# The first fifty microseconds of a Fourier-mixing and ReGLU kernel, put in another order: filter loads, first products, inverse copies

## The chip, the cores and the metric

The kernel runs on one core of a Trainium2 chip. The metric is device time in microseconds (us), the median of the runs; less is better. Three runs of the kernel before gave 865.61, 865.96 and 867.79 us, so its median is 865.96 us. One of its executions was also taken by the hardware profiler; all durations below come from that one.

## What is computed

```python
def _attn_ref(x, filt_r, filt_i):
    X = np.fft.rfft(x, axis=1)              # x: 8 batches, 3008 positions, 256 channels
    F = (filt_r + 1j * filt_i)[None, :, :]  # 1505 frequencies, 256 channels
    Y = X * F
    return np.fft.irfft(Y, n=x.shape[1], axis=1)

def _moe_ref(x, w_gate, w_val, w_out):      # 24064 tokens, 256 -> 1536 -> 256
    gate = np.maximum(x @ w_gate, 0.0)
    val = x @ w_val
    return gate * val @ w_out
```

All inputs and the output are float32.

## The kernel before

**The Fourier part.** The length 3008 is split as 94 x 32 (`N1`, `N2`), and both transforms are small matrix products. For each batch:

- *Stage A* contracts the 94 rows with the table `WA`, in float32. `x` stands in two tiles `XF[0]` and `XF[1]` of 16 columns n2 each, loaded in quarters (`load_x`, L185 to L192; one quarter of a batch is three DMAs of 256 KB). One call of `a_bank` (L260, the matmul is L265) fills one PSUM bank `psA`. Batch 0 uses `a_0` (copies at L277 into `AS0`), batch 1 uses `a_1`. One call of `a_1` is named an *item* below (L651); there are 16 of them, four for each quarter of `x`, and its copies (L290) go to `AS1`.
- A transpose turns the 32 columns n2 into partitions. For batch 0 VectorE does it (`turn_0`, L303, four quarters, the instruction is L300) and the result is the tile `at`. Half of batch 1 goes through DRAM (`store_half`, `load_half`), the other half through VectorE (`turn_1`).
- `fwd(b, i)` (L402) is the second forward product: 16 matmuls fill two banks `psX` (e = 0 and 1). There are six blocks i.
- `product(b, i, e, k)` multiplies such a bank by a filter: k = 0 is the real filter `Ftr` and gives `tt`, k = 1 is the imaginary filter `Fti` and gives `uu`. VectorE does it from PSUM (L422). For three blocks (`ON_POOL`, e = 1 of i = 0, 1, 2) ScalarE copies the bank to `xs` (L419) and GpSimd multiplies (L420).
- `inv(b, q)` (L445) takes the products of blocks 2q and 2q + 1 to four banks `psD`, 64 matmuls for batch 0; there are three. It needs the tables `I2t` and `I2u`, which the kernel makes from `F2` (`make_back_t`, `make_back_u`). For batch 0 the banks are copied into `DS0` (L458) and `turn_d(0)`, `turn_d(1)` (L316) transpose them into `D0`, half of the channels each.
- `item_c(k, h)` (L538) is the last inverse product for 512 tokens and one half h of the channels; its copy (L544 or L546) gives `yT`.

**The feed-forward part** runs over 47 blocks of 512 tokens. `gv` (L555) makes value and gate, ScalarE copies the value (`vsb`, L558), VectorE makes the product with the rectified gate (`prod`, L560), and `o_part` (L576) contracts with `WoT`, copies (L589) and stores (L600). The transforms of batches 1 to 7 are strewn among these blocks by a table of step numbers (`at_step`). The first `gv` needs all of the batch 0 transform.

**What sets the order.** The instructions stand in the order in which the Python calls them; no scheduler moves them. Each engine runs its own queue in order. The eight PSUM banks are handed out in rotation in program order (`bank`, `done`), so an instruction that takes a bank waits for the copy that freed it. DMAs issued by SyncE (SP), and those issued by GpSimd (POOL), rotate over eight semaphores each, so the ninth waits for the first.

**The front.** `load_filters` (L226) issues 16 DMAs on GpSimd in four groups of four: mirrored rows of `Ftr` (L231), mirrored rows of `Fti`, direct rows of `Ftr` (L236), direct rows of `Fti`. After stage A of batch 0, a small DMA `hold` (L647) reads `Ftr[0:2, 4, 0:8]`. It stands in SP's queue ahead of all of batch 1's `x` (L648), so this `x` starts when a mirrored and a direct part of `Ftr` have landed. `first_b` (L472) then mixes forward blocks, products, inverses and items, with filler matmuls (`warm`, L607, 128x512 on a tile of ones). What follows it is short:

```python
    first_b(item)
    ...
    for h in range(2):
        turn_d(h)
    item(7)
    for hh in range(2):
        item_c(0, hh)
    item(3)
    turn_1(0)
```

**The end.** In the last block, `o_part` copies each group of 128 tokens (t = 0 to 3) to a free part of `XF`: VectorE copies t = 1 and 2, and the last group is shared, channels 0 to 127 by VectorE (L585) and the others by ScalarE (L586). Each group is stored by two or three runs of rows, issued by GpSimd (t = 0) or by SP and ScalarE in turn; runs are cut at a multiple of 16 rows into two DMAs (`cut`, L596).

Of the kernel before, what the change touches and what calls it, by code (L numbers as in the profile page):

```python
# [116 lines left out]
def kernel(  # L117
# [18 lines left out]
    W = 512  # L136
# [89 lines left out]
    def load_filters():  # L226

        for src, dst in FILT:
            for c in range(4):
                r, k1, n = 32 * c + 1, 1 + H * c, H - c // 3  # L230
                nc.gpsimd.dma_start(dst[r:r + 31:2, :n, :],  # L231
                                    _ap(src, (N1 - k1) * D, [[N1 * D, 16], [-D, n], [1, D]]))
        for src, dst in FILT:
            for c in range(4):
                r, k1, n = 32 * c, 1 + H * c, H - c // 3
                nc.gpsimd.dma_start(dst[r:r + 31:2, :n, :], _ap(src, k1 * D, [[N1 * D, 16], [1, n * D]]))  # L236
# [31 lines left out]
    def a_0(n2, nn, d0, nd):  # L268

        psA = a_bank(n2, nn, d0, nd)  # L270
        dq = D // 4
        l, q = n2 % NC2, slice(d0 // dq, (d0 + nd) // dq)
        c = n2 // NC2
        dst = AS0.rearrange("p q (l c) e (g f) -> p l c g q e f", c=2, g=2)[:, l:l + nn, c // 2, c % 2]
        src = psA.rearrange("p n (q e f) -> p n q e f", e=dq // 2, f=2)
        for i in range(nd // dq):
            nc.scalar.copy(dst[:, :, q.start + i], src[:, :, i])  # L277
        done(psA)
# [19 lines left out]
    def turn_pairs(dst, src):  # L298

        nc.vector.transpose(dst.bitcast(FP32).rearrange("p k c g -> p c k g"),  # L300
                            src.bitcast(FP32).rearrange("p n c g -> p c n g"))

    def turn_0(q):  # L303
        w = D // 8
        turn_pairs(ats[0][:, :, q * w:q * w + w], AS0[:, q])

# [80 lines left out]

    ON_POOL = ((0, 1), (1, 1), (2, 1))
    ats = {}
# [45 lines left out]
    def inv(b, q):  # L435
# [3 lines left out]
        for m in range(2):  # L439
            for k in range(last + 1):  # L440
                for r in range(2):
                    for c in range(4):
                        for e in range(2):
# [5 lines left out]
                                             tile_position=(32 * c, 64 * e))  # L449
        dst = sb.tile([128, 8, D], BF16, tag="dsb", bufs=3, name="dsb") if b else DS0  # L450
        def out(cs):
            for c in cs:
                copy = nc.vector.tensor_copy if (c % 2 if b else (q, c) in ((1, 3), (2, 0), (2, 1))) else nc.scalar.copy
                if b:
                    copy(dst[:, c:8:4, :], psD[c])
                else:
                    k, g = 4 * q + c // 2, c % 2 * 2
                    copy(dst[:, k:k + 3:2, :, g:g + 2], psD[c].rearrange("p m (f e) -> p m e f", f=2))  # L458
                done(psD[c])
        if not b:  # L460
            return out(range(4))

# [9 lines left out]
    def first_b(item):  # L472

        def products(i, es=(1, 0)):
            for e in es:
                for k in range(2):
                    product(0, i, e, k, pool=(i, e) in ON_POOL)

        for i in range(3):
            fwd(0, i)  # L480
            if i < 2:
                products(i)
        make_back_u()
        products(2)
        warm(3)
        fwd(0, 3)
        products(3, (1,))
        warm(3)
        fwd(0, 4)
# [42 lines left out]
    def item_c(k, h):  # L532
# [35 lines left out]
    def o_part(blk, s, prods):  # L568
# [9 lines left out]
        if s in (5, 11) or last and s % 3 == 2:  # L578
# [3 lines left out]
            else:  # L582
                osb = fs.tile([128, 2, D], FP32, tag="osb", bufs=4)
            if s == 11 and last:
                nc.vector.tensor_copy(osb[:, 1, 0:D // 2], psO[:, 1, 0:D // 2])  # L585
                nc.scalar.copy(osb[:, 1, D // 2:], psO[:, 1, D // 2:])  # L586
            else:
                copy = nc.vector.tensor_copy if last else nc.scalar.copy
                copy(osb[:, t0 % 2:t % 2 + 1], psO[:, t0 % 2:t % 2 + 1])  # L589
# [172 lines left out]
```

## Time and profile before

| What | Value |
|---|---|
| Three runs, median | 865.96 us |
| The profiled execution, its own time | 865.68 us |
| Its span, first to last instruction | 863.8 us (1.9 us lie around it) |
| TensorE matmuls busy | 848.7 us, 98% of the span |
| VectorE, ScalarE, GpSimd busy | 577.8, 494.6, 458.4 us |
| Stage A of batch 0 ends on TensorE | 20.3 us |
| First `gv` matmul | 45.6 us |
| Last matmul ends | 858.2 us |

Engines are written PE (TensorE matmul), PEld (its weight loads), DVE (VectorE), ACT (ScalarE), POOL (GpSimd) and SP (SyncE); a q behind the name (SPq, ACTq) means that the engine issues a DMA. A row of a timeline has the start in us, the length in us, engine, line, operation, output tile <- input tiles, shape, count, and in brackets the idle time before it and what ended it. Rows of equal instructions that follow each other are merged. A row of the chain of waits has start, length, and what the end of the program waited for then. A row of stages has the stretch, its length, then the busy time of PE, PEld, DVE, ACT and POOL with counts, the granted TensorE clock as a share of full speed, the share of time the 16 DMA engines were busy, and GB/s.

### The profile page before, as it was taken

How to read it: one execution, taken by the hardware profiler on the slowest of the kernel's cores; microseconds unless marked ns; L12 is line 12 of the kernel's file. 1: busy time of each engine (PE TensorE's matmuls, PEld its weight loads, DVE VectorE, ACT ScalarE, POOL GpSimd, SP SyncE). 2: the span in 40 equal slices, each digit the busy share in tenths (PEclk: the TensorE clock that was granted, in tenths of full speed). 3: DMA queues.
4: the chain of work that ended last, by engine and by line, in shares of the span. 5: the costliest groups of instructions: out<-in, count | busy, mean ns of one | idle time of the engine just before them, and what ended most of it. 6: DMA issues, size and time to landing. Idle time of an engine off the chain costs nothing.

```text
span 863.8 us, 20396 instructions
## 1 busy us (share of the span) xinstructions
PE 848.7 (98%) x7587; PEld 498.8 (58%) x7704; DVE 577.8 (67%) x863; ACT 494.6 (57%) x904; POOL 458.4 (53%) x496
## 2 busy tenths in 40 slices
PE   9999999999999999999999999999999999999997
PEld 4456655656556555556556655565655656666665
DVE  3878865777657775577765787658865688555553
ACT  5765565555655556555555555555556555555552
POOL 6747890488986765776666756767450023000001
PEclk9999999999999999999999999999999999999999
DMA  9985365334782339633386333762464422611111
GB/s 250 241 164 122 96 158 138 109 113 110 190 183 88 84 87 192 166 98 98 85 208 142 95 103 100 190 151 74 101 130 108 99 58 52 126 43 29 37 35 52
DMA packets 101366, 101.61 MB, mean 118 GB/s; under 512 B 21827, under 2 KB 89955, under 8 KB 99730
## 3 DMA queue, kind: packets, MB, share of 16 engines
q1 hardware_dynamic: 81986, 77.96, 36.1%
q0 software_dynamic: 18928, 21.82, 11.7%
q8 instruction: 61, 1.00, 0.5%
q10 hardware_dynamic: 352, 0.52, 0.2%
q14 instruction: 39, 0.32, 0.1%
HBM read 58.23 MB, written 45.88 MB: 121 GB/s over the span
## 4 chain that ended last, share of the span: by engine, by line
PE 94%; DMA 2%; issue 1%; DVE 1%; ACT 1%; SPq 1%; POOL 0%; DVEq 0%; ACTq 0%
PE psG L555 29%; PE psO L576 28%; PE psV L555 26%; PE psA L265 3%; PE psF L367 3%; PE psY L538 3%; PE psD L445 2%; PE psX L402 1%; DMA XF<-in_x_dram 1%; DMA Abuf<-asb 1%; ACT vsb L558 1%; DVE prod L560 1%; SPq L190 0%; DVE tt L422 0%; DMA out_dram<-osb 0%
## 5 line engine op out<-in xcount | busy, mean ns | idle before, releaser
L560 DVE SCALAR_TENSOR_TENSOR prod<-psG,vsb 128x512 bf16<-128x512 f32 x564 | 389.4, 691 | 235.8 <-ACT vsb L558 231.6
L558 ACT CAST vsb<-psV 128x512 bf16<-128x512 f32 x564 | 332.2, 589 | 225.8 <-PE psV L555 121.1
L576 PE MATMUL psO<-WoT,prod 128*128 128x256 bf16 x2256 | 336.6, 273 | 0.8
L555 PE MATMUL psG<-yT,WgT 128*128 128x512 bf16 x1111 | 331.8, 379 | 5.2
L555 PE MATMUL psV<-yT,WvT 128*128 128x512 bf16 x1030 | 314.9, 380 | 0.1
L576 PEld LDWEIGHTS <-prod 128*128 128x128 bf16 x2256 | 220.6, 98 | 143.4
L555 PEld LDWEIGHTS <-WgT 128*128 128x128 bf16 x1128 | 110.0, 97 | 133.5
L432 POOL TENSOR_TENSOR pp<-tt,uu 128x256 bf16<-128x256 f32 x84 | 60.9, 725 | 170.7 <-DVE uu L422 162.5
L555 PEld LDWEIGHTS <-WvT 128*128 128x128 bf16 x1128 | 100.3, 98 | 37.3 <-issue 25.6
L544 ACT CAST yT<-psY 128x512 bf16<-128x512 f32 x93 | 54.5, 586 | 43.2 <-PE psY L538 42.6
L589 ACT COPY osb<-psO 128x512 f32<-128x512 f32 x92 | 54.1, 588 | 22.1 <-PE psO L576 20.7
L600 POOL DMA_DIRECT2D out_dram<-osb x5 | 2.6, 534 | 119.6 <-ACT osb L589 118.0
L422 DVE TENSOR_TENSOR tt<-psX,Ftr 128x512 f32<-128x512 f32 (+1 forms) x93 | 63.5, 683 | 0.5 <-PE psX L402 0.5
L422 DVE TENSOR_TENSOR uu<-psX,Fti 128x512 f32<-128x512 f32 (+1 forms) x93 | 63.3, 681 | 0.3 <-DMA Fti<-in_filt_i_dram 0.3
L433 POOL TENSOR_TENSOR pp<-tt,uu 128x256 bf16<-128x256 f32 x84 | 60.9, 726 | 0.0
L353 POOL TENSOR_TENSOR fold<-XF 128x1024 f32<-128x1024 f32 x24 | 56.3, 2347 | 5.8 <-DMA XF<-in_x_dram 5.4
L354 POOL TENSOR_TENSOR XF<-XF 128x1024 f32<-128x1024 f32 x24 | 56.4, 2350 | 1.9
L257 POOL CAST scr<-prod 128x8 f32<-128x8 bf16 x19 | 3.6, 190 | 85.8 <-DVE prod L560 71.7
L340 POOL DMA_DIRECT2D XF<-in_x_dram x76 | 45.6, 602 | 2.0 <-issue 1.3
L374 ACT CAST asb<-psF 128x512 bf16<-128x512 f32 x48 | 25.8, 589 | 34.5 <-PE psF L367 34.5
L374 DVE CAST asb<-psF 128x512 bf16<-128x512 f32 x48 | 30.9, 686 | 18.0 <-PE psF L367 18.0
L538 PE MATMUL psY<-M,dCb 96*128 96x94 bf16 (+19 forms) x604 | 37.9, 200 | 0.0
(71 smaller groups left out, 457.8 us busy)
## 6 DMA issues: line engine op xcount, KB each, us to landing
Dbuf<-dsb SPq DMA_DIRECT2D x84, 128.0 KB
dCb<-Dbuf SPq DMA_DIRECT2D x56, 192.0 KB
XF<-in_x_dram POOLq DMA_DIRECT2D x38, 256.0 KB, 6.7
Abuf<-asb SPq DMA_DIRECT2D x96, 96.0 KB
at<-Abuf SPq DMA_DIRECT2D x24, 384.0 KB
XF<-in_x_dram SPq DMA_DIRECT2D x31, 256.0 KB
XF<-in_x_dram POOLq DMA_DIRECT2D x76, 96.0 KB, 5.1
out_dram<-osb SPq DMA_DIRECT2D x69, 94.0 KB
```

What stands on the lines that cost most here:

```text
L353: tt(t, xp[:, 0:2], xp[:, 2:4], op=ALU.add)
L354: tt(xp[:, 2:4], xp[:, 0:2], xp[:, 2:4], op=ALU.subtract)
L374: copy(asf[:, :, q, :], banks[q])
L422: nc.vector.tensor_tensor(p, psX, filt, op=ALU.mult)
L432: nc.gpsimd.tensor_tensor(p[:, 0], tt[:, 0], uu[:, 1], op=ALU.subtract)
L433: nc.gpsimd.tensor_tensor(p[:, 1], tt[:, 1], uu[:, 0], op=ALU.add)
L538: nc.tensor.matmul(psY[:, o:o + w], d_rows(b, n2, h), M1[:, 1, n1:n1 + w] if b == 0 else M1[:NROW, 0, n1:n1 + w], start=True, stop=True)
L544: nc.scalar.copy(dst, psY)
L555: nc.tensor.matmul(pt[:, :W], w[:, h, ft * 128:(ft + 1) * 128], yt[:, h, :], start=(h == 0), stop=(h == 1))
L558: nc.scalar.copy(vsb, psV[:, :W])
L560: nc.vector.scalar_tensor_tensor(prod, in0=psG[:, :W], scalar=0.0, in1=vsb, op0=ALU.max, op1=ALU.mult)
L576: nc.tensor.matmul(psO[:, t % 2], prods[ft][:, t * 128:(t + 1) * 128], WoT[:, ft, :], start=(ft == 0), stop=(ft == NFT - 1))
```

## The change

1. `load_filters` issues all of `Ftr` first (mirrored, direct), then all of `Fti`. The number of DMAs stays at 16.
2. The `hold` becomes two. The first reads one element row of `Ftr` that only the first mirrored DMA writes, and the first quarter of batch 1's `x` stands behind it. The second reads `Fti[0:2, 4, 0:8]` (mirrored and direct), and the other three quarters stand behind that.
3. The last `a_0` copy and the last `turn_0` are cut into two halves.
4. `first_b` runs four forward blocks in a row, then all real products, four items, the imaginary products, and fewer filler matmuls (2 instead of 6). The order on TensorE becomes: fwd 0 to 3, four items, filler, fwd 4, an item, inv 0, fwd 5, two items, inv 1, an item, inv 2. GpSimd does its three `tt` before its three `uu`.
5. The copies of inv 0 and inv 1 are all ScalarE's (before, VectorE did one of the four of inv 1 and two of inv 2). The copies of inv 2 are cut in halves of the channels, with VectorE doing two half copies, and each `turn_d` is issued right behind its half.
6. Behind `first_b` come seven items, `item_c(0, 0)` and `(0, 1)`, and one item (before: seven, then three). Each `yT` copy of block 0 is shared: ScalarE the first 256 tokens, VectorE the others.
7. In the last block, VectorE copies the whole last group, and runs of rows are cut only for t = 2 and 3.

```diff
@@ load_filters
                 nc.gpsimd.dma_start(dst[r:r + 31:2, :n, :],
                                     _ap(src, (N1 - k1) * D, [[N1 * D, 16], [-D, n], [1, D]]))
-        for src, dst in FILT:
             for c in range(4):
@@ a_0
         for i in range(nd // dq):
-            nc.scalar.copy(dst[:, :, q.start + i], src[:, :, i])
+            for e in (slice(0, 16), slice(16, 32)) if (n2, d0) == (24, 3 * dq) else (slice(0, 32),):
+                nc.scalar.copy(dst[:, :, q.start + i, e], src[:, :, i, e])
@@ turn_0
-        turn_pairs(ats[0][:, :, q * w:q * w + w], AS0[:, q])
+        n = 2 if q == 3 else 1
+        for i in range(n):
+            e = slice(i * w // n, (i + 1) * w // n)
+            turn_pairs(ats[0][:, :, q * w + e.start:q * w + e.stop], AS0[:, q, :, e])
@@ inv
+        if not b:
+            w = D // 4
+            for h in range(2) if q == 2 else (0,):
+                for c in range(4):
+                    k, g = 4 * q + c // 2, c % 2 * 2
+                    e = slice(h * w, h * w + w) if q == 2 else slice(0, 2 * w)
+                    copy = nc.vector.tensor_copy if (q, h) == (2, 0) and c > 1 else nc.scalar.copy
+                    copy(DS0[:, k:k + 3:2, e, g:g + 2], psD[c].rearrange("p m (f e) -> p m e f", f=2)[:, :, e])
+                if q == 2:
+                    turn_d(h)
+            for c in range(4):
+                done(psD[c])
+            return
...
@@ first_b
+        for i in range(4):
+            fwd(0, i)
+        for k in range(2):
+            for i in range(3):
+                product(0, i, 1, k, pool=True)
         for i in range(3):
-            fwd(0, i)
-            if i < 2:
-                products(i)
+            product(0, i, 0, 0)
+        for e in (1, 0):
+            product(0, 3, e, 0)
+        item(2)
+        for i in range(3):
+            product(0, i, 0, 1)
         make_back_u()
-        products(2)
-        warm(3)
-        fwd(0, 3)
-        products(3, (1,))
-        warm(3)
+        item(2)
+        warm(2)
+        for e in (1, 0):
+            product(0, 3, e, 1)
         fwd(0, 4)
-        item(2)
-        products(3, (0,))
+        item(1)
         inv(0, 0)
         fwd(0, 5)
-        products(4)
-        item(2)
-        products(5)
+        for i in (4, 5):
+            for e in (1, 0):
+                for k in range(2):
+                    product(0, i, e, k)
+            if i == 4:
+                item(2)
         place_own()
         inv(0, 1)
-        item(2)
+        item(1)
         inv(0, 2)
@@ item_c
-        if h == 0 or k:
+        if k:
             nc.scalar.copy(dst, psY)
         else:
-            nc.vector.tensor_copy(dst, psY)
+            nc.scalar.copy(dst[:, :W // 2], psY[:, :W // 2])
+            nc.vector.tensor_copy(dst[:, W // 2:], psY[:, W // 2:])
@@ o_part
-            if s == 11 and last:
-                nc.vector.tensor_copy(osb[:, 1, 0:D // 2], psO[:, 1, 0:D // 2])
-                nc.scalar.copy(osb[:, 1, D // 2:], psO[:, 1, D // 2:])
-            else:
...
-                    cut = w // 16 * 16 if last and not pool else 0
+                    cut = w // 16 * 16 if last and t > 1 else 0
@@ the order of the front
-    hold = sb.tile([2, 8], BF16, tag="hold", bufs=1)
-    nc.sync.dma_start(hold, Ftr[0:2, 4, 0:8])
-    load_x(1, sp, ((0, 0, 2 * q), (0, 2 * q, 4 * q), (1, 0, 2 * q), (1, 2 * q, 4 * q)))
+    for done_by, parts in ((Ftr[1:3:2, 0, 0:8], ((0, 0, 2 * q),)),
+                        (Fti[0:2, 4, 0:8], ((0, 2 * q, 4 * q), (1, 0, 2 * q), (1, 2 * q, 4 * q)))):
+        hold = sb.tile([2, 8], BF16, tag="hold", bufs=2)
+        nc.sync.dma_start(hold[:done_by.shape[0]], done_by)
+        load_x(1, sp, parts)
...
-    for h in range(2):
-        turn_d(h)
     item(7)
     for hh in range(2):
         item_c(0, hh)
-    item(3)
+    item(1)
```

More of the change, by code (lines that the diff above doesn't have):

```diff
@@ L386, in load_at_tiled @@
                               _ap(Abuf[b], rr * N2 * NG * D, [[NG * D, 32], [1, NG * D]]))
-    ON_POOL = ((0, 1), (1, 1), (2, 1))
     ats = {}
@@ L449, in inv @@
                                              tile_position=(32 * c, 64 * e))
-        dst = sb.tile([128, 8, D], BF16, tag="dsb", bufs=3, name="dsb") if b else DS0
+        if not b:
[11 more added lines that the diff above has]
+            return
+        dst = sb.tile([128, 8, D], BF16, tag="dsb", bufs=3, name="dsb")
         def out(cs):
             for c in cs:
-                copy = nc.vector.tensor_copy if (c % 2 if b else (q, c) in ((1, 3), (2, 0), (2, 1))) else nc.scalar.copy
-                if b:
-                    copy(dst[:, c:8:4, :], psD[c])
-                else:
-                    k, g = 4 * q + c // 2, c % 2 * 2
-                    copy(dst[:, k:k + 3:2, :, g:g + 2], psD[c].rearrange("p m (f e) -> p m e f", f=2))
+                copy = nc.vector.tensor_copy if c % 2 else nc.scalar.copy
+                copy(dst[:, c:8:4, :], psD[c])
                 done(psD[c])
-        if not b:
-            return out(range(4))
         def rest():
@@ L472, in first_b @@
     def first_b(item):
[L474 to L477, printed above, removed]
-        for i in range(3):
-            fwd(0, i)
-            if i < 2:
-                products(i)
-        make_back_u()
-        products(2)
-        warm(3)
-        fwd(0, 3)
-        products(3, (1,))
-        warm(3)
+        for i in range(4):
[3 more added lines that the diff above has]
+                product(0, i, 1, k, pool=True)
+        for i in range(3):
+            product(0, i, 0, 0)
[4 more added lines that the diff above has]
+            product(0, i, 0, 1)
+        make_back_u()
+        item(2)
+        warm(2)
+        for e in (1, 0):
+            product(0, 3, e, 1)
         fwd(0, 4)
-        item(2)
-        products(3, (0,))
+        item(1)
         inv(0, 0)
         fwd(0, 5)
-        products(4)
-        item(2)
-        products(5)
+        for i in (4, 5):
[4 more added lines that the diff above has]
+                item(2)
         place_own()
         inv(0, 1)
-        item(2)
+        item(1)
         inv(0, 2)
@@ L583, in o_part @@
                 osb = fs.tile([128, 2, D], FP32, tag="osb", bufs=4)
-            if s == 11 and last:
[L585 to L589, printed above, removed]
+            copy = nc.vector.tensor_copy if last else nc.scalar.copy
+            copy(osb[:, t0 % 2:t % 2 + 1], psO[:, t0 % 2:t % 2 + 1])
             done(psO)
```

## The prediction, on record before the changed kernel ran

> **What bounds the kernel now.** I read the stages first, to find where TensorE is not full.
>
> ```profile
> 20.30:26.80 6.50, 5.18 (x185) 2.49 (x187) 5.71 (x9) 5.60 (x11) 3.10 (x3) 1.00 0.96 269
> 45.60:858.00 812.40, 806.34 (x7102) 478.98 (x7215) 551.40 (x829) 464.42 (x840) 427.54 (x450) 1.00 0.46 111
> 861.50:863.80 2.30, 0.00 (x0) 0.00 (x0) 0.00 (x0) 0.00 (x0) 0.00 (x0) 0.57 0.01 4
> ```
>
> From the first `gv` (45.6) to 858 PE is busy for 806.3 of 812.4 us; the rest is about 1% (records missing from a trace look the same), and the change doesn't touch this stretch. It can only move it, and cut what lies behind it. So the question is when the first `gv` starts, and how long the tail is. Next the chain of waits of the front:
>
> ```profile
> 20.29 0.71 PE psI L207 x48
> 21.05 0.58 SPq L190
> 21.69 4.97 DMA XF<-in_x_dram
> 26.66 0.14 issue
> 26.80 1.96 PE psA L265 x4
> 28.75 1.05 PE psD L445 x64
> ```
>
> After stage A (20.3) the chain runs over the load of batch 1's `x`: PE waits until 26.8 for its first item. Then the timelines of the engines, rows from several of them (PE; POOL; DVE; ACT):
>
> ```profile
> 23.05 0.82 PE L611 MATMUL psJ<-junk 128*128 128x512 bf16 x2
> 25.20 0.28 PE L402 MATMUL psX<-at,F 64*32 64x256 bf16 x1 [0.98 <-issue]
> 25.42 0.82 PE L611 MATMUL psJ<-junk 128*128 128x512 bf16 x3
> ```
> ```profile
> 16.16 1.97 POOL L236 DMA_DIRECT2D Ftr<-in_filt_r_dram  x4 [1.51 <-DMA Ftr<-in_filt_r_dram]
> 23.70 1.15 POOL L420 TENSOR_TENSOR tt<-xs,Ftr 128x512 bf16<-128x512 f32 x1 [3.64 <-ACT xs L419]
> ```
> ```profile
> 18.68 3.51 DVE L300 STREAM_TRANSPOSE at<-AS 128x1024 f32<-128x1024 f32 x3
> 23.67 0.69 DVE L422 TENSOR_TENSOR uu<-psX,Fti 128x512 bf16<-128x512 f32 x1 [0.26 <-DMA Fti<-in_filt_i_dram]
> 37.75 4.60 DVE L300 STREAM_TRANSPOSE dCb<-AS 128x2048 f32<-128x2048 f32 x2
> ```
> ```profile
> 29.78 2.06 ACT L458 CAST AS<-psD 128x512 bf16<-128x512 f32 x4 [0.41 <-PE psD L445]
> ```
>
> Between 23.05 and 26.8 PE has filler and gaps only around two short forward blocks: about 3 us that items could fill. From 36.3 on PE is full again. Sixteen items are 15 us of the front (7 in a row take 6.0 us, 0.86 each).
>
> **The change, part by part.** Times are on the clock of the profiled run.
>
> *Turn halves: 0.* The four quarters follow each other on DVE from 17.5 to 22.2 (1.17 each), so the last begins at 20.95 because DVE is busy, not because ACT is late. Halving gains nothing, and costs at most 0.1, hidden behind the `psI` matmuls, which end at 22.2.
>
> *Early quarter of x.* POOL's wait of 1.51 at 16.16 is for the first mirrored `Ftr`: the first hold is released then, not at 19.65. Its issue takes 0.75 (row of L647), and three issues follow by 18.8. The first and third x DMA landed some 4.9 us after issue before, so 23.2 at the latest. PE would take the first item when fwd 3 is done and ACT has freed a bank by its first `xs` copy (ends 23.6). So items 1 to 4 run 23.65 to 27.1 instead of beginning at 26.8.
>
> *What the quarter displaces.* Between 16.16 (first of 16 filter DMAs landed) and 23.67 (last) one lands every 0.50 us. Three x DMAs of 256 KB at the best rate of any slice (426 GB/s) take 1.85 us of the same DMA engines. `Ftr` is now the first eight: 16.2 + 3.5 + 1.85 = 21.5 at worst, needed at 22.7. The last `Fti` lands at 23.67 + 1.85 = 25.5. Five real products stand ahead of the first `uu` on DVE (22.73 + 5 x 0.60 = 25.73), and three on POOL (23.70 + 3 x 1.12 = 27.06). So the wait of 0.26 goes, with 0.2 to spare.
>
> *Second hold.* It needs the thirteenth filter DMA: 22.2 by the pace now, 24.0 with the quarter. Plus 0.75 and three issues of 0.6, the third DMA of the second quarter goes out at about 26.1 and lands between 2.5 (the first x DMAs of the run on idle queues) and 4.97 later: 28.6 to 31.1. I take 28.6, because by then nearly all filters have landed. Behind it in SP's queue are only x loads, and the items of quarters 3 and 4 come after 36. Item 5 waits for it on PE, and fwd 5, inv 0 and all later stand behind item 5.
>
> *inv 0.* It needs POOL's `uu` of block 1, now fifth instead of fourth: 23.70 + 5 x 1.12 = 29.3 instead of 28.2; and banks that ACT frees after its `I2u` and item copies, at about 29.25. Item 5 ends at 29.45. So inv 0 runs 29.5 to 30.55, against 28.68 to 29.75: **0.8 us later**, but with five items done instead of two.
>
> *inv 1, inv 2.* Before, inv 1 started 2.6 us behind the end of inv 0 (ACT's first copy, then two items); the same two items stand there now: 33.15 to 34.2. One item (0.86) instead of two: inv 2 runs 35.05 to 36.1, against 35.26 to 36.27. DVE's last product ends at 33.6 (33.9 before) and is no bound.
>
> *Copies by halves.* ACT does all four copies of inv 1 (4 x 0.48, the 2.06 row) and an item's (0.65) and is free at 36.7; two half copies (0.27 apart, 0.37 long, as the `asb` rows) end at 37.3. `turn_d` is 2 x 2.3 by its row: 37.3 to 41.9. Before it ended at 42.35 and held `item_c`. Now PE's seven items end later: 36.1 + 6.0 = 42.1. **The transposes are no longer last; PE is.**
>
> *item_c and what follows.* `item_c` 42.1 to 42.65; one item to 43.5, where three took until 45.6. ACT still copies item 15 until 43.0, then the `yT` halves at 0.27 apart; the built order shows that DVE's half waits for ACT's half, each about 0.4 (0.42 is the 128x256 copy of the tail). So the second half of `yT` is ready at 44.0 to 44.1, and `gv` runs without a hole from about 43.95 instead of 45.6: **-1.65 us**. With side by side copies it would be 43.6 (-2.0); with an ACT that is 0.5 later, 44.4 (-1.2). The weights were issued at 31.2 to 35.9 and this place on POOL does not move.
>
> [...]
>
> *The tail.* The timeline of the end:
>
> ```profile
> 858.25 0.29 DVE L585 COPY XF<-psO 128x128 f32<-128x128 f32 x1 [0.88 <-PE psO L576]
> 858.92 0.27 ACT L586 COPY XF<-psO 128x128 f32<-128x128 f32 x1 [5.32 <-DMA out_dram<-osb]
> 859.21 0.96 ACTq L600 DMA_DIRECT2D out_dram<-XF  x2
> ```
>
> ACT is still issuing stores when its half of the last copy is due, so the last stores start at 859.2. One copy on DVE takes 0.42 (rows of t = 1 and 2): done at 858.67. The last stores start 0.5 earlier, and ACT has one issue less (0.45) before them. **-0.5 us**, between -0.2 (ACT's queue late again) and -0.7.
>
> *Sum.* -1.65 - 0.5 = -2.15 on a run of 865.68 us, that is 863.5. The median is 0.28 above the profiled run, so 863.8 for the median.
>
> **The rivals.**
>
> *A. The x pieces come late, the gain shrinks.* If the second quarter lands at 30.1 instead of 28.6, item 5 and all behind it move 1.5; the front then gains 0.15 and the tail 0.5: 865.3. For: before, issue to landing was 4.97. Against: that was with filters ahead in the queues. The same order of loss, 0.9, comes if the first quarter lands at 25.3 as before (1.65 late, 0.75 of it absorbed by the hole before item 5): 864.7. Together 20%.
>
> *B. Slower: the hold on the imaginary filters empties PE.* Place: item 5. Each us by which the second quarter lands later than 28.6 is paid in full; at 30.75 the whole gain is gone. If it lands at 31.2 or later, PE has stood still since fwd 4 (27.8) for 3.4 us. In the last stage shown above PE stops at 858.2 and the granted clock is 1.00 up to 861.5 and falls to 0.57 on average after it. So a hole of 3.3 us also costs the clock; if it stays at half for as long again, 1.7 us more. -2.15 + 2.7 + 1.7 = +2.2: 868.2. Six fillers became two, which speaks for it; the hole of 0.98 before, with the clock at 1.00, speaks against it. 6%.
>
> [...]
>
> *C. More than I count.* The second quarter is there at 27.8, inv 0 starts at 29.3, the `yT` copies finish 0.3 earlier, and the tail gives 0.7: -2.15 - 0.2 - 0.3 - 0.2 = -2.85, 863.1. 27%.
>
> *D. The holes only move.* `item_c` starts at 42.1 against 42.4 before; nearly all the gain is the two items that no longer stand behind it. If ACT lags PE by two items there (0.65 each), `yT` is ready at 45.3, the front gains 0.35 and the tail 0.5: 865.1. Against: in the seven items of before ACT was busy 0.6 to 0.65 of every 0.86 and kept pace. 2%.
>
> **How the numbers follow.** Forecast 863.8, 45%, from 863.3 to 864.5 by the bounds of `yT` and tail. A 20%, B 6%, C 27%, D 2%. About 0.3%, 2.6 us, is what a measurement here can tell from no change, so faster by more means under 863.4: most of C and the lower edge of the forecast, 34%. Slower by more means over 868.6, part of B: 4%. Within: 62%. The range leaves out B and the ends of A and C: 862.6 to 865.6.
>
> **What would show it.** First item on PE at 23.6; POOL's first `uu` at 27.1 without a wait; PE idle before item 5 up to 0.8; inv 0 later than before; `turn_d` done before PE's seven items; first `gv` at 43.9; last stores from 858.7. Wrong if DVE's first `uu` waits for `Fti`, if `gv` starts after 45, or if the clock of a stage in the front is under 1.

## The result, and the profile after

The changed kernel takes **870.19 us** (median of 7 runs, 868.95 to 873.06) beside 866.21 us for the kernel before (7 runs): ratio 1.0043, 95% interval 1.0026 to 1.0060. It is slower, by about 0.4%. Measured once more (e5 below) the ratio is 1.0033, from 1.0022 to 1.0044. The forecast of 863.8 us and its range, 862.6 to 865.6, missed it.

The span of the profiled execution is 868.3 us, 4.51 more than before. It falls into three pieces: the first `gv` starts at 48.54 instead of 45.59 (**+2.95**, forecast -1.65); from there to the end of the last matmul it takes 812.70 instead of 812.62 (+0.08); the tail behind that is 7.09 instead of 5.61 (**+1.48**, forecast -0.5).

The stages of the profile after (start:end, length, then busy us of PE, PEld, DVE, ACT, POOL, each with its count, PE's granted clock, DMA share, GB/s):

```profile
20.30:26.80 6.50, 3.85 (x166) 1.97 (x164) 5.57 (x9) 4.09 (x10) 3.40 (x5) 0.99 0.83 198
26.80:36.30 9.50, 9.05 (x109) 4.06 (x110) 6.24 (x11) 5.81 (x13) 7.42 (x10) 0.83 0.73 229
45.60:862.00 816.40, 815.61 (x7234) 480.40 (x7232) 553.36 (x833) 466.66 (x846) 428.63 (x452) 1.00 0.46 111
```

PE was to be busier in the first of them and is busy 3.85 us instead of 5.18: the fillers are gone and no item has taken their place. DMA moves 198 GB/s instead of 269. In the second stage the clock is 0.83 on average: one stretch of it ran at half clock.

The chain of waits of the front, after:

```profile
10.88 5.92 DMA Ftr<-in_filt_r_dram
...
16.81 0.80 SPq L659
...
18.90 7.96 DMA XF<-in_x_dram
26.86 0.14 issue
27.00 5.22 PE psA L264 x8
```

The first hold is released at 16.81 (forecast 16.16), but the third `x` DMA takes 7.96 us and lands at 26.86 (forecast: "23.2 at the latest").

In the traces of before and after each DMA of `x` and of a filter has 16 updates of its semaphore, and what waited for it went on behind the last one. Of the third DMA's 16, 15 had come by 25.04 and the last came at 26.86, 0.14 ahead of item 1. The last imaginary filter is alike (15 by 25.96, the last at 27.45), and from 25.6 to 27.1 the mean share of the 16 DMA engines is 0.04, less than one engine. So in this execution about 1.8 us of the wait are one late update; in e5, the same kernel, the DMA landed at 24.92. A 16 KB instruction packet was in transfer just before, from 24.38 to 25.49. Whether it made the difference stays open: in e3 one at nearly the same time (24.33 to 25.28) left no such delay.

The PE rows (start, busy, line; the idle time before them in brackets):

```profile
27.00 5.22 PE L264 MATMUL psA<-XF,WA 128*128 128x512 f32 x8 [2.82 <-DMA XF<-in_x_dram]
32.93 1.13 PE L264 MATMUL psA<-XF,WA 128*128 128x512 f32 x2
40.80 6.28 PE L264 MATMUL psA<-XF,WA 128*128 128x512 f32 x14
48.54 0.71 PE L569 MATMUL psV<-yT,WvT 128*128 128x512 bf16 x2
```

Item 1 starts at 27.00, no earlier than before (26.80), and four items take 5.22 us where the row of seven gives 0.86 each. The clock record is 0.5 for 3.41 us from 26.7 on, the end of the hole of 2.82 (24.18 to 27.00). Item 5 starts at 32.93 instead of 28.6, and all later steps keep that lateness of about 4.5: from there on the order works as worked out (`turn_d` is done before PE's seven items, one item follows `item_c`).

The products, and SP's issues:

```profile
27.73 3.08 DVE L424 TENSOR_TENSOR uu<-psX,Fti 128x512 bf16<-128x512 f32 x5 [1.33 <-DMA Fti<-in_filt_i_dram]
26.68 0.67 SPq L659 DMA_DIRECT2D hold<-Fti  x1
27.46 6.44 SPq L190 DMA_DIRECT2D XF<-in_x_dram  x9
```

VectorE waits 1.33 us for the imaginary filter, the sign that the forecast named for its being wrong. The second hold is released at 26.68, when the thirteenth filter DMA lands (again one update, 1.65 us behind the other 15), and the second quarter is issued only from 27.46 on.

### The profile page after: what moved, and what is told of

Its sections match the earlier page's. It is cut to its first block, busy times and chain, and to the rows that moved or that the text cites. A ratio compares the mean times of both kernels' runs of the same rounds, so it can differ in the third digit from the quotient of the medians.

```text
span 868.3 us, 20515 instructions
## 1 busy us (share of the span) xinstructions
PE 855.8 (99%) x7700; PEld 499.6 (58%) x7700; DVE 576.8 (66%) x864; ACT 495.1 (57%) x910; POOL 458.6 (53%) x496
## 4 chain that ended last, share of the span: by engine, by line
PE 95%; DMA 2%; SPq 1%; POOL 0%; issue 0%; ACT 0%; POOLq 0%
PE psV L569 29%; PE psG L569 28%; PE psO L590 28%; PE psF L370 3%; PE psY L551 3%; PE psA L264 2%; PE psD L447 2%; DMA XF<-in_x_dram 2%; PE psX L404 1%; DMA Ftr<-in_filt_r_dram 1%; SPq L190 1%; POOL out_dram L610 0%; SPq L659 0%; ACT osb L599 0%; ACT AS L459 0%
## 5 line engine op out<-in xcount | busy, mean ns | idle before, releaser
L569 PE MATMUL psV<-yT,WvT 128*128 128x512 bf16 x1128 | 336.0, 379 | 0.0
L569 PE MATMUL psG<-yT,WgT 128*128 128x512 bf16 x1128 | 335.3, 379 | 0.0
```

Source lines behind the costliest of these rows:

```text
L569: nc.tensor.matmul(pt[:, :W], w[:, h, ft * 128:(ft + 1) * 128], yt[:, h, :], start=(h == 0), stop=(h == 1))
```

## The experiments

All ran in five rounds beside the kernel before (e16 and e17 in three). "Shifted code" is explained at e6. Columns: third DMA of the first quarter lands; item 1 starts; PE's `issue` stall at 24 to 27; last `Fti` lands; inv 0 and the first `gv` start; clock in the front; tail; median; ratio to before with interval. The landings are from the trace's semaphore records, and each row has one profile: 0.3 us between two rows can be chance. The ratios are those on record; they are not the quotients of the two medians.

| kernel | x | item 1 | stall | Fti | inv 0 | gv | clock | tail | median | ratio |
|---|---|---|---|---|---|---|---|---|---|---|
| before | 26.66 | 26.80 | 0.98 | 23.55 | 28.68 | 45.59 | 1.0 | 5.61 | | |
| after | 26.86 | 27.00 | hidden | 27.45 | 33.99 | 48.54 | lost | 7.09 | 870.19 | 1.0043 |
| e1 copy | 27.00 | 27.13 | 1.24 | 24.02 | 29.02 | 45.98 | 1.0 | 5.45 | 866.90 | 0.9993 (0.9979-1.0007) |
| e2 uncut | 26.65 | 27.36 | 1.15 | 24.95 | 29.28 | 46.29 | 1.0 | 5.90 | 867.59 | 1.0000 (0.9986-1.0014) |
| e3 front | 24.44 | 24.57 | 1.28 | 25.09 | 32.45 | 46.92 | 1.0 | 5.16 | 868.16 | 1.0009 (0.9996-1.0021) |
| e4 work order | 27.86 | 28.00 | hidden | 24.89 | 35.59 | 50.07 | lost | 5.5 | 869.20 | 1.0021 (1.0009-1.0032) |
| e5 after | 24.92 | 25.06 | 1.21 | 26.87 | 32.70 | 47.17 | 1.0 | 7.12 | 869.65 | 1.0033 (1.0022-1.0044) |
| e6 e3 + code | 24.69 | 24.83 | none | 26.40 | 31.83 | 46.54 | 1.0 | 5.8 | 869.54 | 1.0030 (1.0018-1.0042) |
| e7 e6 + x | 24.45 | 24.59 | none | 29.43 | 32.69 | 48.43 | lost | 5.7 | 868.71 | 1.0031 (1.0013-1.0049) |
| e8 e3 + x | 25.23 | 25.36 | 1.67 | 28.23 | 35.72 | 50.19 | lost | 5.3 | 869.10 | 1.0026 (1.0015-1.0038) |
| e9 both tail edits | 27.69 | 27.83 | 0.77 | 25.25 | 31.37 | 48.33 | lost | 5.88 | 867.36 | 1.0001 (0.9990-1.0012) |
| e10 e6 + item 5 | 23.99 | 24.12 | none | 25.85 | 28.53 | 45.00 | 1.0 | 5.69 | 866.74 | 1.0004 (0.9984-1.0023) |
| e11 e6 + fillers | 24.72 | 24.86 | none | 25.89 | 32.01 | 46.51 | 1.0 | 5.7 | 868.96 | 1.0021 (1.0005-1.0037) |
| e12 loads | 25.64 | 30.04 | 2.85 | 27.26 | 33.10 | 49.95 | lost | 5.63 | 870.21 | 1.0031 (1.0021-1.0042) |
| e13 e3 + item 5 | 25.01 | 25.15 | 1.21 | 26.77 | 32.70 | 48.80 | lost | 5.54 | 868.67 | 1.0012 (0.9993-1.0031) |
| e14 before + code | 28.95 | 29.09 | none | 25.12 | 32.64 | 49.58 | lost | 5.70 | 868.19 | 1.0008 (0.9988-1.0028) |
| e15 e10 + copy | 24.98 | 25.11 | none | 25.81 | 29.50 | 45.96 | 1.0 | 5.0 | 868.82 | 1.0018 (0.9997-1.0039) |

The median of before was 866.76 beside e1 to e4, 866.84 beside e5 to e8, 867.04 beside e9 to e12 and 866.6 beside e13 to e15.

### The parts: tail, front, order of work, loads (e1 to e4, e12)

e1: the kernel before, the last copy whole on VectorE, runs cut as before. e2: the kernel before, `cut` only for t > 1, the last copy split. e3: the changed kernel with the tail of before. e4: e3 with the filter order and the one hold of before, so the new order of work alone.

```diff
 # e3: the tail of before in the changed kernel
-            copy = nc.vector.tensor_copy if last else nc.scalar.copy
+            if s == 11 and last:
...
-                    cut = w // 16 * 16 if last and t > 1 else 0
+                    cut = w // 16 * 16 if last and not pool else 0
```

> The kernel before, with one part of the change at its end alone: VectorE copies the whole last group of the last block; the stores stay cut at 16 rows. Theory (the copy helps, the uncut stores harm): the last stores start 0.5 us earlier than the 0.9 us behind the last matmul seen before, so 0.3 to 0.5 us less than the kernel before, 865.8. Rival (the whole copy on one engine is what made the tail of the changed kernel longer): 0.5 to 1.5 us more.

> The kernel before, with the other part of the tail alone: the runs of rows of the group t = 1 are stored whole (94 and 26 rows as one DMA each), the last copy stays shared. Theory: the 94 row store takes about 4 us as in the profile of the changed kernel (issued 859.14, its semaphore complete at 863.2), and the last small store, which rotates to the same semaphore, waits for it: 1 to 2 us more than the kernel before, 867.2 to 868.2. Rival (the cut is harmless, fewer issues help): 0 to 0.5 us less.

> The changed kernel with the end of the kernel before (its shared last copy and all its cuts); the whole new front stays. Theory (two separate losses, front and tail): 1.5 to 2 us less than the changed kernel, so about 868.3, still 2 us over the kernel before; PE waits 2 to 3 us for the first quarter of x, and the granted clock is 0.5 for 3.4 us behind that. Rival (the front is harmless on most executions and the tail is all): about 864.5.

> As the one before, and the filter order and the single hold of the kernel before put back: new order of products, items and copies on the old loads. Theory (the loss of the front comes from the early quarter of x amid the filters, not from the new order of work): faster than the new front by 1.5 to 3 us. The first item still waits for x until about 26.7, with no filler before it, so PE stands still from 24.2 to 26.7, 2.5 us, under the 3.3 us at which the clock fell at the end of the kernel before; if the clock holds, gv starts at 45 to 45.5 and the time is 865.5 to 866. Rival 1 (the new order itself empties PE, whatever the loads): the clock falls here too, and it is at 868 like the new front. Rival 2: DVE waits for Fti as before and nothing else matters: 866.2.

Neither edit of the tail by itself moves the time, so neither the gain that I expected of e1 nor the loss of 1 to 2 us of e2 is there. The new front alone costs 1.3 us of `gv` by its profile and 1.4 by its median; the interval just reaches 1. e3's time came as expected, yet its profile kept the clock, which I had expected it to lose. And the new order of work on the old loads, which I had expected to be faster than e3, has a median 1.0 higher (e4). So the early quarter isn't all that loses: without it PE has nothing between fwd 3 and item 1, stands for 4.19 us and runs 6.83 us at half clock. In the timed runs, too, the mean granted clock is under 0.998 in 10 of 12 for e4 and in 3 of 12 for e3. The front of e3, where the clock was kept, shows the other two waits:

```profile
24.57 0.67 PE L264 MATMUL psA<-XF,WA 128*128 128x512 f32 x1 [0.43 <-DMA XF<-in_x_dram]
26.52 3.27 PE L264 MATMUL psA<-XF,WA 128*128 128x512 f32 x7 [1.28 <-issue]
31.42 1.10 PE L264 MATMUL psA<-XF,WA 128*128 128x512 f32 x2 [0.84 <-DMA XF<-in_x_dram]
```

One is an `issue` stall of 1.28 inside item 1, the other the second quarter, which lands at 31.29. Why it is so late is in the DMA share of 20 to 28 us, 40 slices of 0.2 us, of before and then of e3:

```profile
DMA  4997999298798995969964894696998939937969
```
```profile
DMA  6999999999999999999979000000000091937939
```

A packet counts in the slice in which it begins. Before, `x` is already queued behind the filters and no slice is empty. With the second hold hardly a packet begins from 24.4 to 26.4 (those begun earlier, the last an instruction packet, end at 25.28): SP learns at 24.44 that the filter is there, issues (0.67 for the hold, then 0.6 for each DMA), and the bytes of `x` begin to move 2 us behind that release.

e12 is the counterpart: the new loads in the kernel before, with its own order of work.

```diff
-        for src, dst in FILT:
             for c in range(4):
...
+    for done_by, parts in ((Ftr[1:3:2, 0, 0:8], ((0, 0, 2 * q),)), (Fti[0:2, 4, 0:8], (...)))
```

> The kernel before with the new order of the filters and the two holds alone; its own order of work. Theory (the loads cost by themselves: each x DMA among the filters makes the imaginary ones later): the last imaginary filter lands at 25 to 27 instead of 23.55, the first imaginary product on VectorE 1.4 to 3 us later than 23.67, inv 0 at 30 to 31.8 instead of 28.7, gv at 47 to 48.5, time 1.5 to 3 us above before. Rival (the loads gain, the new order of work loses): item 1 by 25, inv 0 by 28.7, gv at 45.6 or earlier, time not above before.

The theory held in direction, and every figure went beyond the range that I gave. VectorE's first imaginary product starts at 27.54 instead of 23.67, and the `issue` stall grows to 2.85 us:

```profile
27.17 0.28 PE L401 MATMUL psX<-at,F 64*32 64x256 bf16 x1 [2.85 <-issue]
```
```profile
27.54 0.69 DVE L421 TENSOR_TENSOR uu<-psX,Fti 128x512 bf16<-128x512 f32 x1 [4.05 <-DMA Fti<-in_filt_i_dram]
```

So the loads lose by themselves (median 3.2 us above before) and the order of work loses by itself (2.4), while both together lose 1.4 (e3). That the sum is less than either part is not shown beyond doubt: the intervals of e3 and e4 overlap, e12 was timed in another session, and e4 and e12 lost the clock in their profiles.

### The instructions, and x without the second hold (e5 to e8)

In the profiles of before, e1, e2 and e3 the stall stands behind exactly 214 recorded matmuls, whatever these are. A packet of 16 KB on the instruction queue lies beside it (window of before, 22.7 to 23.8; packets, MB, share):

```profile
q8 instruction: 1, 0.02, 5.1%
```

By the trace's records it lands at 23.68 (before) and 25.28 (e3), and PE goes on at 25.20 and 26.52, 1.5 and 1.2 us behind. In e6, 64 short fillers ahead move that place of the program to an earlier time:

```diff
-    warm(18, 256)
+    warm(12, 256)
+    warm(40, 32)
...
         a_0(n2, 4, h * D // 2, D // 2)
+    warm(30, 32)
```

e7 and e8 issue the second quarter right behind the first, e7 with the shifted code, e8 without; e5 is the changed kernel again.

```diff
-    ... ((Ftr[1:3:2, 0, 0:8], ((0, 0, 2 * q),)),
-         (Fti[0:2, 4, 0:8], ((0, 2 * q, 4 * q), (1, 0, 2 * q), (1, 2 * q, 4 * q))))
+    ... ((Ftr[1:3:2, 0, 0:8], ((0, 0, 2 * q), (0, 2 * q, 4 * q))),
+         (Fti[0:2, 4, 0:8], ((1, 0, 2 * q), (1, 2 * q, 4 * q))))
```

> The changed kernel once more, beside the next three on one chip. Theory (the front loses by itself, the tail and the clock add to it): first item at 24.5 to 27, first gv at 46.5 to 48.5, tail 0.3 to 1.5 us longer than before; time 1.5 to 4 us above before. Rival (the first measurement was a chance of its day): within 1 us of before.

> The new front with the tail of before, and 64 more small filler matmuls ahead of and in stage A, so that the program position at which PE stalled (behind 214 matmuls, in four profiles, beside a 16 KB instruction packet on q8) is passed at another place. Theory (PE waits there for its next block of instructions): no 1.28 us 'issue' stall in the first item; items 1 to 4 run without a hole from 24.6 to 28.1 instead of to 29.8; then PE waits about 1.3 us longer before item 5, because the second quarter still lands at 31.3, so gv stays at 46.9 (within 0.3) and the time is that of the new front, 868.2. Rival (the stall belongs to the moment, 25.2 us, or to PSUM): a stall of about 1.2 us is still there at 24 to 26.5.

> As the kernel with the shifted code, and the second quarter of x is issued right behind the first (one hold for both). Theory (late instructions and the late second quarter are what the forecast missed): items 1 to 4 run from 24.6 to 28.1, item 5 by 28.7, inv 0 at 30.3 to 30.8 instead of 32.45, gv at 44.8 to 45.3, time about 866 (gain of 1.6 to 2.1 us on the new front alone, 0 to 0.6 better than before). Rival (the filters, displaced by three more x DMAs, make POOL's imaginary products late by about 1.85 us): inv 0 at 32 or later, gv at 46.5 or later, nothing gained.

> The new front with the tail of before and the second quarter issued right behind the first, the code not shifted. Theory (two separate waits): the stall in item 1 stays (items 1 to 4 end at 29.8 to 30), item 5 follows without a wait for x, inv 0 at about 31.2, gv at about 45.7, 1.2 us earlier than the new front alone: time about 867. Rival (the second quarter is hidden by the stall or by the filters anyway): gv at 46.9.

e6 (PE):

```profile
24.83 3.67 PE L264 MATMUL psA<-XF,WA 128*128 128x512 f32 x8 [1.13 <-ACT xs L421]
30.80 1.10 PE L264 MATMUL psA<-XF,WA 128*128 128x512 f32 x2 [1.52 <-DMA XF<-in_x_dram]
```

The stall is gone and four items run through; a packet now comes at 16.0 (and a further one at 25.5 to 26.4, beside which PE has no hole). So the stall belongs to that place of the program and not to the moment (1.28 us in e3, none in e6), and the packet of 16,384 bytes moves with it. That PE waited there for its next instructions is my reading; no record says for which engine the packet is. But `gv` gains only 0.4, because item 5 now waits 1.52 us for `x`: the waits lie behind each other, and removing one uncovers the next. Its median is 869.54 and not 868.2 as expected; its profile loses 3 us between `gv` and the last matmul (last section), which points to a cause elsewhere.

e5 came as expected: in its profile, the slowest of its eight runs, `gv` is 1.6 us later than before, the tail 1.5 longer, and 2.5 are lost between `gv` and the last matmul.

e7 went to the rival. The last `Fti` lands at 29.43, and PE waits in fwd 4, because `psX` banks are freed by VectorE's imaginary products:

```profile
30.44 0.27 PE L404 MATMUL psX<-at,F 64*32 64x256 bf16 x1 [1.97 <-DVE uu L424]
```

inv 0 is at 32.69, no earlier than in e3. e8's profile lost the clock for 6.83 us, so it can't test the size I gave; its median is no better than e3's either. In both, bytes that come earlier for `x` come later for `Fti` (e8 28.23 against 25.09 in e3, e7 29.43 against 26.40 in e6).

### Item 5, the clock, the best front (e10, e11, e13, e14, e15)

Before, inv 0 needs the filters and one quarter of `x`; changed, it needs two quarters, only because item 5 stands ahead of it. e10 is e6 with that item behind fwd 5:

```diff
         fwd(0, 4)
-        item(1)
         inv(0, 0)
...
             if i == 4:
-                item(2)
+                item(3)
```

e11 is e6 with `warm(4)` ahead of item 1 and `warm(7)` for `warm(2)`. e13 is e3 with item 5 moved, e14 the kernel before with the shifted code, e15 is e10 with e1's copy.

> The new front with the shifted code and the tail of before, and item 5 moved from ahead of inv 0 to behind fwd 5 (three items in a row there). Theory (inv 0 waits for the second quarter of x only through item 5, which stands ahead of it on PE): inv 0 at 30.2 to 30.8 instead of 31.8, gv at 45.0 to 45.6 instead of 46.5, time about 1 to 1.5 us under the kernel with the shifted code. Rival (inv 0 is held by POOL's imaginary products and ACT's I2u in any case): inv 0 at 31.3 or later and gv at 46.2 or later.

> The new front with the shifted code and the tail of before, with four more fillers (1.1 us) ahead of item 1 and five more (1.3 us) ahead of fwd 4, in PE's two waits. Theory (part of the loss is the clock, which PE loses by chance in those waits): the mean granted clock is 0.998 or more in at least 10 of 12 runs, against 3 of 12 without them, gv within 0.4 of 46.5, and the median falls by 0.5 to 1.5 us. Rival (the clock isn't lost there, or the fillers delay as much as they save): as many runs under 0.998 as without them, median within 0.5 us of it or above.

> The new front with the tail of before and item 5 behind fwd 5, the code not shifted. Theory (now nothing but the instructions holds PE there, so the stall costs its whole length): 'issue' stall of 1.2 to 1.9 us in the first item, inv 0 about 1.2 us later than with the shifted code (28.5 to 29.7 there), gv at 45.9 to 46.5 against 45.0, median 1 us or more above 866.7. Rival (ACT's copies or POOL's products hold inv 0 anyway): gv at 45.0 to 45.4 in spite of the stall.

> The kernel before with the 64 additional small fillers ahead of and in stage A, nothing else. Theory (there the stall lies beside the wait for x of batch 1 and costs nothing): no 'issue' stall at 24.2, item 1 still at 26.6 to 27.1 when x lands, gv within 0.3 of 45.6, time within 0.6 us of before. Rival (the stall costs before, too): gv at 44.6 to 45.0 and time 0.6 to 1 us under before.

> The kernel with item 5 moved and the code shifted, and the last copy whole on VectorE (the stores cut as before). Theory (front -0.6 us, copy -0.16 us by their profiles): gv at 45.0 to 45.4, tail 5.3 to 5.6, median 0.3 to 1 us under before where the clock is kept; runs that lose it lie 3 to 5 us higher, so that the interval still reaches 1. Rival (the gain is lost later, in the waits for the loads of batches 2 and 3): time at or above before.

e10 (PE):

```profile
24.12 3.70 PE L264 MATMUL psA<-XF,WA 128*128 128x512 f32 x8
28.53 0.29 PE L447 MATMUL psD<-tt,I2t 32*64 32x256 bf16 x2
31.40 2.84 PE L264 MATMUL psA<-XF,WA 128*128 128x512 f32 x6 [0.24 <-ACT AS L459]
45.00 0.71 PE L568 MATMUL psV<-yT,WvT 128*128 128x512 bf16 x2
```

From 22.7 on PE has only 0.9 us of holes and 0.6 of fillers, inv 0 starts even earlier than I expected, and `gv` is at 45.00, 0.59 earlier than before. That is the only front that beats the one of before by its profile; its median (866.74 beside 867.04) cannot be told from it. e13 shows the price of the stall and of a stretch at half clock together (0.56 on average from 26.7 to 30.1; `gv` 48.80, median 2.1 above the before beside it); one profile with the clock lost doesn't separate them. e14: the stall is gone and nothing is gained, as the theory had it; but in its profile `x` itself came 2 us late and the clock was lost, so `gv` says nothing there, and its median is 1.6 us above before where I had expected 0.6 at most. e15 starts `gv` at 45.96 and has the shortest tail (5.0), but its median is 868.82, 2.2 above the before beside it, where the theory had 0.3 to 1 under. Its runs fall in two groups: six with a mean granted clock of 0.998 or more take 865.4 to 868.2 us, six with less take 869.4 to 870.8. No version beats before in a way that these runs can show, and that e10's front mends the loss rests on one profile and its median, which e15 didn't repeat.

e11 kept the clock in the front, with `gv` as in e6. By the mean granted clock of the timed runs, 9 of 12 have 0.998 or more, against 3 of 12 for e6 (I had expected at least 10); the median is 0.6 lower (in another session, beside a before that was 0.2 higher), but that mean also holds the fall behind the last matmul (0.57 on average in the last 2.3 us of before), so this points to the theory and doesn't prove it.

### The tail (e9, e16, e17)

e9 has both tail edits on the kernel before. e16 is e9 with the hold DMA ahead of `x` issued twice, e17 the changed kernel with one more such DMA.

> The kernel before with both edits of the tail (last copy whole on VectorE; the runs of 94 and 26 rows of the second tile stored in one piece), nothing else. Alone they measured -0.16 and +0.3 us of tail in the profile; in the changed kernel, measured twice, the tail is 1.5 us longer than before. Theory (the order of the lanes decides: the front of the changed kernel issues one DMA more, so the uncut store lies in another lane there): here tail 5.7 to 5.9 us, time within 0.5 us of before. Rival (the two edits together cost what neither does alone): tail 7.1 us, time about 1.5 us above before.

> The kernel before with both edits of the tail (which alone gave a tail of 5.88 us), and the small hold DMA ahead of x of batch 1 issued twice, so that every later DMA of SP and ACT lies one lane further, as in the changed kernel. Theory (lanes): tail 7.0 to 7.2 us, with the uncut store of 94 rows and the last store of 14 rows in the lanes that they have in the changed kernel. Rival (something else of the front): tail 5.7 to 6.0.

> The changed kernel with one more small DMA behind its loads of x, which rotates the lanes by one more. Theory (lanes): the tail leaves 7.1 us, by 0.4 us or more in either direction. Rival: tail 7.0 to 7.2 again.

e9's tail is 5.88 us, 0.3 above before and not 1.5; e16's is 6.53, so rotating the lanes costs 0.65 more, less than I had said; e17 stays at 7.03, against the theory. These are single profiles. Eleven kernels with the tail of before lie between 5.16 and 5.82, so the 0.3 of e9 can hardly be told from chance, while the 7.03 to 7.12 of after, e5 and e17 lie well clear. By time e9 and e16 cannot be told from before (e16: median 867.13, ratio 0.9971 to 1.0014); e17 is slower, like after (869.81, 1.0023 to 1.0047).

What SP waits for behind the last matmul, in after and then in e9 (line: us in total, times, longest; the higher line number is the end of the program):

```profile
SPq L767 <- DMA out_dram<-XF: 1.9, 1, 1.9
SPq L610 <- DMA out_dram<-XF: 1.5, 1, 1.5
SPq L767 <- DMA out_dram<-osb: 0.8, 1, 0.8
```
```profile
SPq L596 <- DMA out_dram<-XF: 1.6, 1, 1.6
SPq L753 <- DMA out_dram<-XF: 1.2, 3, 0.7
```

In both the last store (14 rows, SP) waits 1.5 to 1.6 us for the lane, that is the semaphore, of an older store: the uncut one of 26 rows, done 2.3 us behind the last matmul in after and 2.4 in e9. It is issued at 2.3 to 2.4 and not at 1.44 as before. The store ahead of it (2 rows, ACT) waits for the uncut one of 94 rows. This has only two late semaphore updates, 1.89 and 1.96 us behind the last matmul; cut into 80 and 14 rows (before), the 80 rows have 16, the last at -0.1. Why the uncut one is later isn't shown.

The semaphore records split each tail in two, the last landing of a store and what the program does behind it:

| us behind the last matmul | before | e9 | e16 | after | e5 | e17 |
|---|---|---|---|---|---|---|
| the last store has landed | 3.90 | 4.71 | 4.72 | 5.40 | 5.43 | 5.42 |
| from there to the end | 1.71 | 1.17 | 1.81 | 1.69 | 1.69 | 1.61 |

So the uncut stores cost 0.8 us of landing (4.82 in e2, where they alone were changed; 3.7 to 4.2 in the eleven kernels with the tail of before), and in e9 the lanes give 0.5 of it back. At its end the program asks for one lane after the other (in after, the late one until 5.41 and seven more from 5.49 to 6.19 us behind the last matmul). In before, after and e16 the late lane is among the first, and the others are asked behind it; in e9 it is the last. The other 0.7 of after, e5 and e17 is again one update: the last update of each of the last five stores comes 0.65 to 0.8 us behind the one before it, and in e9 and e16 at most 0.1. An 8 KB instruction packet lies at 2.3 to 2.6 us in those three and behind 5.3 in e9 and e16. That it is the cause is not shown.

## Why the prediction was wrong, point by point

- *Early quarter of x*: failed. "The first and third x DMA landed some 4.9 us after issue before, so 23.2 at the latest" took a latency from a time when the filters were nearly through. Among them it was 5.5 to 8.0, landing at 24.0 to 26.9 in the eleven profiles with the new order of work and an early quarter. That is +0.5 to +3.4 on item 1. The upper end, after itself, holds the one late update of 1.8 us, which nothing in the forecast allowed for.
- *A stall read as a gap.* The row `[0.98 <-issue]` lay in my quoted lines, and I counted it as time that items could fill. It was a wait, for instructions in my reading; it moved to what stands at that place now and grew to 1.2 to 1.7 us.
- *Second hold*: failed, and it is the step that decides where the clock is kept. "I take 28.6": 29.7 to 32.7 by the trace (31.29 in e3, 31.54 in e5). I worked out the issue at 26.1 (26.4 in e3), but took the shortest latency, 2.5, "because by then nearly all filters have landed". By the semaphore records that was the very first `x` DMA of the run alone; the next ones took 3.1 us and more. In e3 the quarter's first two DMAs took 2.95 and 3.19 on engines that the hold had emptied, and the third, which decides, took 4.9. Why the third took longer isn't shown; a 16 KB instruction packet lies beside it (28.4 to 29.4), and where the code was shifted (e6, e10, e11, e15) the third took 3.2 to 4.2, elsewhere 4.0 to 5.2. In after the hold's release added to it: the third DMA went out at 28.64 instead of 26.1 and landed at 32.68.
- *Rival B* was this mechanism, at 6%: "Each us by which the second quarter lands later than 28.6 is paid in full". In e3 that is 2.7 on -1.65, +1.05; measured +1.33. Its clock loss came too, but at item 1, behind holes of 1.4 to 2.8 us and not 3.3. Its 1.7 us took a half clock that lasts as long as the hole: an estimate, for no row of before shows how long it lasts; in after it is 3.41 us, behind a hole of 2.82. With it the changed kernel's profile has +2.95. In after item 5 had no wait of its own left: PE, at half clock for a part, was busy with the four items until 32.2 and with fwd 4 until 32.9. The chance was too low: B's landing at 31.2 lies a tenth from my own bound of 31.1.
- *What the quarter displaces*: the price was right in kind (1.85 us forecast; last `Fti` 25.1 to 27.5 against 23.55, 1.5 to 3.9). In e3 it landed within the forecast and VectorE didn't wait. The wait of 1.33 in after, for which 0.2 us were to spare, stands behind the late update.
- *inv 0*: not 0.8 later but 3.8 (e3) to 5.3 (after), through item 5. e10 confirms this.
- *Copies by halves, item_c and gv*: the mechanism held. From item 5's end to `gv` I worked out 14.5 us; in after it is 14.5 (34.06 to 48.54), in e3 14.4. Nothing of the miss is there. VectorE's half of the `yT` copies did wait for ScalarE's (1.54 us at 48.07).
- *Tail*: wrong sign. VectorE's copy was done 0.5 earlier, as forecast; but I didn't cost the other edit of the same lines, the runs that are no longer cut: the last store waited for their lane, was issued 0.9 later, and the last landing came 1.5 later. "-0.5" became +1.48. Some 0.8 of that is shown to come with the uncut stores (e2, e9, e16); the other 0.7, the late update, stays open.

## What to carry to other kernels

Before filling a hole, ask what it is: the `issue` stall here, with a packet on the instruction queue beside it, moved with the program (1.28 us in e3, none in e6) and was no free time. The transfer put ahead of others was paid by these (last `Fti` at 25.1 to 27.5 instead of 23.55), so count for the first consumer behind the change all bytes that it needs, and leave nothing in its queue that needs more; a hold that keeps a queue orderly also drains it (2 us here without bytes). What waited for a DMA went on behind its last update, so one late update moved the whole landing (1.8 us in after). And an edit that only changes the shape of a store needs a cost of its own (0.8 us of landing here).

## What the hardware showed that I had not expected

- **PE stalls beside a packet of instructions.** The 16 KB packet landed at 23.7 to 24.2 in before, e1 and e2, and at 25.3 to 26.4 where `x` ran among the filters (after, e3, e5, e8, e12), but also at 25.1 in e4, which has the old loads; PE went on 1.2 to 1.6 us behind it. The stall was 0.77 to 2.85 us, always at one place of the program (behind 214 to 216 recorded matmuls; a few records are missing from a trace). That the data ahead of it delays the packet is my reading of the groups; no run took the data away.
- **The clock's stretches are multiples of 3.41 us.** Its records up to the end of a half-clock stretch last 3.41, 6.83, 20.48, 23.89 and (e7) 27.31 us, one, two, six, seven and eight times 3.41. Holes of 1.40 and 1.21 in 3.4 us lost it in e13; 1.45 and 1.21 kept it in e5. What decides between the two isn't shown. The changed kernel lost the clock in one profile (after, a hole of 2.82) and kept it in the other (e5, 2.66 in two holes). The front of before can lose it too (e9, `gv` at 48.33).
- **A second hazard far from the change.** The stretch from `gv` to the last matmul took 812.5 to 815.6 us. Most of the difference is one or two waits of PE at the reloaded `at` tile, at 370 and 580 us, here in e1, where only the tail was changed:

```profile
580.76 0.63 PE L402 MATMUL psX<-at,F 64*32 64x256 bf16 x31 [1.43 <-DMA at<-Abuf]
```

 It is absent in before, after and eleven others, and 0.3 to 2.4 us in e3, e5, e6, e10 and e12. Whether the front makes it more frequent stays open; it is one reason why a front that is 0.6 us better by its profile can't be told from no change.
